# Transposes in two row halves, values in three pieces, a sixth query/key buffer and a new list

## The chip, the cores and the metric

The kernel runs on one core of a Trainium2 chip. The metric is the device time of one execution in microseconds (us), as the median of several runs; lower is better.

## The reference, cut to what matters

Causal attention on 4 batches of 12 heads (448 tokens, head size 64), and behind it a mixer: a product over tokens with a ReLU, added to x, then a product over channels with a ReLU, added again. All in 32-bit floats.

```python
def _attn_ref(q, k, v):
    scores = scale * np.matmul(q, k.transpose(0, 1, 3, 2))
    mask = np.triu(np.ones((seq, seq), dtype=bool), k=1)
    scores = np.where(mask, -1000000000.0, scores)
    scores = scores - np.max(scores, axis=-1, keepdims=True)
    attn = np.exp(scores)
    attn = attn / (np.sum(attn, axis=-1, keepdims=True) + 1e-09)
    return np.matmul(attn, v).astype(np.float32)

def _moe_ref(x, w_tok1, w_tok2, w_ch1, w_ch2):
    xt = x.transpose(0, 2, 1)
    h = np.maximum(xt @ w_tok1, 0.0) @ w_tok2
    u = x + h.transpose(0, 2, 1)
    h2 = np.maximum(u @ w_ch1, 0.0) @ w_ch2
    return (u + h2).astype(np.float32)
```

The 48 heads are taken as 24 pairs; x is 448 x 768 for a batch, w_tok1 448 x 256, w_ch1 768 x 1536.

## The kernel before, in words

**Attention.** For each of the 24 pairs: load q, k and v (SP's queue), transpose q and k in blocks (DVE), scores (TensorE, L958, both heads of the pair on row and column halves of the array), mask and maximum (DVE, L980), exponent with its sum (ACT, L992), scale by the reciprocal (POOL, DVE or ACT, L628 and L626), transpose the probabilities, multiply by v (TensorE, L1146 and, for the last 64 rows of keys, L1153, here called tips), and copy the result to u (`utile`, transposed: head size on the partitions). Rows of queries are handled in blocks of 64, grouped into four rounds (`ROUND`), two of which make a row group (`RG`). `probs` holds the probabilities of a round.

**Transposes.** The first ten pairs (`TURN = 10`) transpose their probabilities on TensorE (`by_tensor`, L1049): per round three or four squares of 128 x 128 into one PSUM bank, then one copy to `pt` (ACT or DVE). Two rounds hold their heads crossed and use an identity with its halves swapped, `across_ident`. The other 14 pairs use DMA transposes (`by_dma`, L1101), which this change leaves as they are. `xturn` (L1195) transposes u back for the product over tokens: per pair four squares into one bank, then a copy to `xh` and the remainder to `xl`.

**Mixer.** Products in fp32r with each operand split in a leading part and a remainder, three matmuls for one: over tokens L1243 and L1276, over channels L1326 and later L1654, L1725 and L1745. Products over channels of earlier batches stand between the attention of later ones.

**What sets the order.** `Plan` takes every piece of work as a job with a cost per engine, what it needs and what it holds. `emit` walks through a planned time and gives each engine the ready job with the lowest rank. The rank is taken from a table by name and pair (`PLACES`), the engine, where there is a choice, from another (`CHOICE`). PSUM banks are lent by kinds with a share each (`SHARE`: "s" scores, "t" transposes, "a" values, "m" mixer). Where TensorE has nothing ready in the first 75 us of planned time and was not busy enough just before, the plan puts in a filler, a matmul on the mask into a bank nobody reads (L854). Each engine then runs its list strictly in order, so a filler's time is spent whatever the others do. Where the way that TensorE's array is divided changes from one job to the next (`tiled`), the plan adds `SWITCH` ns.

**Buffers.** `kq` holds raw and transposed q and k, in five buffers; a load on SP's queue (L880) needs a free one.

## Time and profile before

| what | us |
|---|---|
| median of 3 runs | 548.14 (546.58 to 548.21) |
| the profiled execution, whole | 546.4 |
| its span, first to last instruction | 544.6 |
| TensorE busy | 535.3 |
| VectorE (DVE) busy | 426.5 |
| ScalarE (ACT) busy | 327.2 |
| GpSimd (POOL) busy | 147.8 |

Busy means that at least one instruction of the engine runs. TensorE's matmuls overlap: one's recorded duration is from its start to its last result, and the next starts long before that, so the pace is the distance of starts. Line numbers are those of the kernel before; in the changed kernel L958 is L957, L1049 is L1051, L1146 is L1167, L1153 is L1176, L1195 is L1213, L1326 is L1355 and L854 is L853.

### The profile page before, as it was taken

Reading aid. Unit: us, or ns where it says so; the run is one execution under the profiler, and the core shown is the slowest. Engines: PE = TensorE matmul, PEld = TensorE weight load, DVE = VectorE, ACT = ScalarE, POOL = GpSimd, SP = SyncE. Lnnn points to the kernel's source line nnn. Section 1 sums busy time; section 2 is a strip of 40 time slices with the busy share of each in tenths; the row PEclk is TensorE's granted clock in tenths of the full one; section 3 lists DMA queues with packets and bytes.
Section 4 is the critical chain, followed back from the end, with each engine's and each line's share of the span. In section 5 each row is a group of like instructions: output and inputs, shape, how many; then the busy total and the mean of one; then the engine's idle time right before and its main releaser. Section 6 shows DMA issues by size and latency. Waiting matters only on the chain.

```text
span 544.6 us, 11173 instructions
## 1 busy us (share of the span) xinstructions
PE 535.3 (98%) x3908; PEld 460.4 (85%) x3913; DVE 426.5 (78%) x1048; ACT 327.2 (60%) x786; POOL 147.8 (27%) x186
## 2 busy tenths in 40 slices
PE   8999999999999999999999999999999999999996
PEld 3678887888879888888877989999999999999995
DVE  5999888988796898687868798369987758476764
ACT  4999988889997796788758853154232314131300
POOL 2355844345233222203213010062201112221200
PEclk9999999999999999999999999999999999999999
DMA  6777777899899999999899745248632111212138
GB/s 111 148 172 148 180 173 163 215 201 176 188 190 194 199 213 178 200 179 177 193 191 196 190 130 161 77 109 162 130 89 73 45 60 57 65 52 88 29 62 142
DMA packets 231784, 77.69 MB, mean 143 GB/s; under 512 B 206000, under 2 KB 221232, under 8 KB 231728
## 3 DMA queue, kind: packets, MB, share of 16 engines
q1 hardware_dynamic: 220112, 75.37, 63.4%
q10 hardware_dynamic: 11616, 1.61, 1.7%
q8 instruction: 31, 0.51, 0.4%
q14 instruction: 25, 0.20, 0.2%
HBM read 49.15 MB, written 14.94 MB: 118 GB/s over the span
## 4 chain that ended last, share of the span: by engine, by line
PE 87%; DMA 6%; ACT 3%; SPq 2%; DVE 1%; issue 1%; ACTq 0%; POOL 0%; DVEq 0%; POOLq 0%
PE ps L1326 29%; PE ps L1745 14%; PE ps L1654 12%; PE ps L958 7%; PE ps L1146 6%; PE ps L1243 5%; PE ps L1276 5%; PE ps L1049 3%; PE ps L1725 3%; DMA out_dram<-kq 2%; PE ps L1195 2%; DMA pt<-prob 2%; SPq L880 2%; PE ps L1153 2%; PE ps L854 1%; ACT prob L992 1%
## 5 line engine op out<-in xcount | busy, mean ns | idle before, releaser
L1393 DVE TENSOR_TENSOR u<-ps,u 128x448 f32<-128x448 f32 x118 | 72.6, 618 | 38.9 <-PE ps L1745 25.5
L992 ACT ACTIVATE prob<-prob,stat 128x256 f32<-128x256 f32 (+6 forms) x168 | 83.6, 501 | 12.5 <-DVE stat L980 12.2
L637 POOL TENSOR_TENSOR wl<-wf,wh 128x768 fp32r<-128x768 f32 x22 | 41.4, 1883 | 99.1 <-ACT wh L626 71.4
L980 DVE CUSTOM_DVE_ANT_0 prob<-ps,mask 128x128 f32<-128x128 f32 (+6 forms) x168 | 63.2, 414 | 4.9 <-PE ps L958 4.5
L1326 PE MATMUL ps<-uh,wh 128*128 128x448 f32 x144 | 54.4, 378 | 0.0
L1326 PE MATMUL ps<-gh,wl 128*128 128x448 f32 x144 | 52.9, 367 | 1.2 <-POOL wl L637 1.2
L1326 PE MATMUL ps<-gh,wh 128*128 128x448 f32 x144 | 53.5, 372 | 0.0
L1326 PE MATMUL ps<-uh,wl 128*128 128x448 f32 x144 | 52.7, 366 | 0.1
L1326 PE MATMUL ps<-ul,wh 128*128 128x448 f32 x144 | 52.6, 365 | 0.0
L1326 PE MATMUL ps<-gl,wh 128*128 128x448 f32 x144 | 52.6, 365 | 0.0
L626 ACT ACTIVATE wh<-wf 128x768 fp32r<-128x768 f32 x26 | 21.6, 843 | 51.0 <-PE ps L1745 22.6
L628 POOL TENSOR_SCALAR prob<-prob,stat 128x384 f32<-128x384 f32 (+6 forms) x62 | 35.5, 580 | 60.5 <-DVE stat L1014 46.8
L958 PE MATMUL ps<-kq,kq 64*64 64x128 f32 (+5 forms) x768 | 46.6, 359 | 1.3 <-DVE stat L1011 0.8
L958 PEld LDWEIGHTS ps<-kq,kq 64*64 64x64 f32 x768 | 26.6, 133 | 20.8 <-issue 12.6
L632 ACT COPY pt<-pt 128x384 uint16<-128x384 uint16 (+3 forms) x45 | 36.1, 851 | 5.2 <-DMA pt<-prob 5.2
L1146 PE MATMUL ps<-pt,vraw 128*64 128x128 f32 (+1 forms) x384 | 37.2, 333 | 0.1
L1146 PEld LDWEIGHTS ps<-pt,vraw 128*64 128x64 f32 x384 | 23.7, 136 | 11.7 <-issue 2.4
L628 POOL TENSOR_SCALAR wh<-wf 128x768 fp32r<-128x768 f32 x16 | 14.0, 876 | 70.2 <-DVE wf L696 57.2
L686 ACT ACTIVATE wf<-wraw 128x768 f32<-128x768 f32 x24 | 21.9, 911 | 17.8 <-DMA wraw<-in_moe_w_ch_dram 17.4
L632 ACT COPY prob<-prob 128x1024 uint16<-128x1024 uint16 (+1 forms) x33 | 31.0, 950 | 2.0 <-DMA pt<-prob 1.1
L992 ACT ACTIVATION_READ_ACCUMULATOR prob<-prob,stat 128x1 f32 x168 | 32.0, 191 | 0.0
L1745 PE MATMUL ps<-u,wh 128*128 128x448 f32 x108 | 30.7, 365 | 0.0
(217 smaller groups left out, 1436.4 us busy)
## 6 DMA issues: line engine op xcount, KB each, us to landing
wraw<-in_moe_w_ch_dram SPq DMA_DIRECT2D x24, 768.0 KB, 5.5
wf<-scratch SPq DMA_DIRECT2D x30, 384.0 KB, 3.4
scratch<-wf SPq DMA_DIRECT2D x24, 384.0 KB, 4.4
vraw<-in_v_dram SPq DMA_DIRECT2D x48, 96.0 KB, 2.8
kq<-in_k_dram SPq DMA_DIRECT2D x60, 56.0 KB, 3.2
kq<-in_q_dram SPq DMA_DIRECT2D x56, 56.0 KB, 3.9
gh<-in_k_dram SPq DMA_DIRECT2D x36, 56.0 KB, 2.6
gl<-in_q_dram SPq DMA_DIRECT2D x36, 56.0 KB, 2.5
```

The lines of the kernel that those rows point to most:

```text
L628: eng[e].tensor_scalar(dst, src, scale, 0.0, op0=ALU.mult, op1=ALU.add)
L632: nc.scalar.copy(out, in_)
L637: eng[e].tensor_tensor(dst, a, b, op=ALU.subtract)
L958: nc.tensor.matmul(scores[n].tile[lanes, to:at], lhsT=qe.tile[LANES[j], c * QC:(c + 1) * QC], rhs=ke.tile[LANES[j], slice(*keys)], start=T ...
L980: nc.vector.tensor_tensor_reduce(out=part(c, r), in0=ps.tile[:, at:at + wide(c)], in1=mask[:, S - QC:S + P] if c == 2 else mask[:, S - wid ...
L992: nc.scalar.activation(part(c, r), part(c, r), AF.Exp, bias=stat.tile[:, 0, AT[c]:AT[c] + 1], scale=-1.0, accum_out=stat.tile[:, 1, AT[c]: ...
L1146: nc.tensor.matmul((low if c == 1 else ps).tile[LANES[j], c * QC:(c + nq) * QC], lhsT=s.tile[:, kb, j], rhs=view[:, o, 1 - j if c in MIXED ...
L1243: nc.tensor.matmul(ps.tile[:, :PART], lhsT=w[:, c, m * P:(m + 1) * P], rhs=x.tile[:, c, :], start=(n == 0), stop=(n == len(work) - 1),)
L1326: nc.tensor.matmul(ps.tile[:, :S], lhsT=x.tile[:, at_:at_ + P], rhs=y, start=(n == 0 and i == 0), stop=(n + 1 == w[2] and i == 2),)
L1393: eng[e].tensor_tensor(u, ps.tile[:, :S], u, op=ALU.add)
L1654: nc.tensor.matmul(ps.tile[:, :S], lhsT=l()[:, t * P:(t + 1) * P], rhs=r, start=(t == 0 and n == 0), stop=(t == half - 1 and n == 2),)
L1745: nc.tensor.matmul(ps.tile[:, :S], lhsT=l.tile[:, t * P:(t + 1) * P], rhs=r.tile, start=(n == 0), stop=(n == 3 * len(fs) - 1),)
```

## The change

**Transposes.** `by_tensor` now transposes a row group at a time, seven squares. Each square is two transposes of 64 rows and 128 columns, one on the upper and one on the lower row half of the array, into two PSUM banks; the crossed identity goes, since a half's place in `pt` now tells which head it is. Two copies follow, one for each bank, 448 columns each. `xturn` does the same for two pairs of u at once: eight squares, 16 half transposes, two banks, then two copies and two remainders. "t" may hold four banks.

**Values.** The job of a pair's values becomes three jobs: two of matmuls and one of tips. For the first ten pairs the new layout of `pt` cuts the columns differently (`PIECES`): eight matmuls per head and pair with two or one block of 64 queries each, where there were four with four or two.

**Buffers and plan.** `kq` gets a sixth buffer. `tiled` tells four ways of dividing the array apart instead of two, `SWITCH` is 95, and both tables are new. Of them the diff shows one row.

```diff
-    "by_tensor.flip": {0: (36, 40, 63, 72), 2: (77, 89, 92, 118), 4: (122, 141, 156, 166), 6: (170, 185, 207, 225),
...
+    "by_tensor.flip": {0: (39, 60), 2: (81, 88), 4: (128, 151), 6: (186, 195), 8: (259, 283), 10: (363, 374), 12:
+        (388, 421), 14: (470, 489), 16: (534, 549), 18: (544, 569)},
...
-    LEAD, SWITCH, RING, LANDS = 1400.0, 100.0, 128.0, (1400.0, 1000.0)
+    LEAD, SWITCH, RING, LANDS = 1400.0, 95.0, 128.0, (1400.0, 1000.0)
...
-    BUFS = {"wraw": 1, "wf": 2, "wh": 2, "wl": 2, "kq": 5, "vraw": 2, "vend": 2, "pt": 2}
+    BUFS = {"wraw": 1, "wf": 2, "wh": 2, "wl": 2, "kq": 6, "vraw": 2, "vend": 2, "pt": 2}
...
-    SHARE = {"s": 4, "t": 2, "a": 2, "m": 3, "w": 5}
+    SHARE = {"s": 4, "t": 4, "a": 2, "m": 3, "w": 5}
...
-    across_ident = const.tile([P, P], F32, name="across_ident")
-    for o in (0, P // 2):
-        nc.gpsimd.tensor_copy(across_ident[:, o:o + P // 2], ident[:, P // 2 - o:P - o])
...
+    FLAT = (7, 0)
+    PIECES = ((0, 0, 3, 3, 2, 4, 3), (0, 0, 4, 1, 2, 0, 11), (1, 0, 1, 1, 1, 6, 1), (1, 0, 2, 1, 1, 3, 1),
+              (0, 1, 3, 3, 2, 5, 3), (0, 1, 4, 1, 2, 1, 11), (0, 2, 5, 1, 1, 13, 1), (0, 2, 6, 1, 1, 9, 1))
+    TIPS = {15: 10, 9: 2}
...
-        prev = None
-        for r, cs in enumerate(ROUND):
+        for rg, at in zip(RG, FLAT):
...
-            ps = share("t")
...
-                        across_ident if r in CROSS else ident,
...
+            for r in rg:
+                for c in ROUND[r]:
...
+            both = share("t"), share("t")
+            squares = [(r, o) for r in rg for o in range(WIDTH[r])]
+            n = len(squares)
+            def flip(e, both=both, squares=squares):
+                for ps in both:
+                    bank(ps)
+                for k, (r, o) in enumerate(squares):
+                    for ps, rows in zip(both, LANES):
+                        nc.tensor.transpose(
+                            ps.tile[:, k * QC:(k + 1) * QC], probs[r].tile[rows, o * P:(o + 1) * P], ident[rows, rows]
+                        )
+            a = plan.job(
+                {"pe": 50.0 + 58.0 * n}, flip, norms, [*both, pt] + [probs[r] for r in rg], rank, tiled=3, turn=True
+            )
+            for h, ps in enumerate(both):
+                def evac(e, h=h, ps=ps, at=at, n=n):
+                    if pt.tile is None:
+                        make(pt, [P, 2, 2 * n, QC], F32)
+                    copy(e, pt.tile[:, h, at:at + n], ps.tile[:, :n * QC].rearrange("p (o q) -> p o q", q=QC))
+                done.append(plan.job({"act": act_ps(n * QC), "dve": dve1(n * QC)}, evac, [a], [ps, pt], rank))
...
+        banks = ps, low
+        flat_ = g < TURN
+        def chunks(n, j):
+            if flat_:
+                which, kb, c, step, nq, o, stride = PIECES[n]
+                out = banks[which].tile[LANES[j]].rearrange("p (c q) -> p c q", q=QC)[:, c:c + step * (nq - 1) + 1:step]
+                rhs = pt.tile[:, 1 - j if c in OVER else j, o:o + stride * (nq - 1) + 1:stride]
+                return kb, out, rhs
+            kb, o, c, nq = SUMS[n]
+            view = pt.tile.rearrange("p o (j q) -> p o j q", j=2)
+            return kb, banks[c == 1].tile[LANES[j], c * QC:(c + nq) * QC], view[:, o, 1 - j if c in MIXED else j]
+        def tip(o, c, j, half):
+            if flat_:
+                return pt.tile[LANES[half], 1 - j if c in OVER else j, TIPS[o]]
+            return pt.tile.rearrange("p o (j q) -> p o j q", j=2)[LANES[half], o, 1 - j if c in MIXED else j]
+        first_of = (0, 2) if flat_ else (0, 1)
...
-        for part in (range(2), range(2, 4)):
+        for part in ((range(4), range(4, 8)) if flat_ else (range(2), range(2, 4))):
...
+                        kb, to, rhs = chunks(n, j)
+                        nc.tensor.matmul(to, lhsT=s.tile[:, kb, j], rhs=rhs, start=(n in first_of), stop=False)
+            prev = plan.job(
+                {"pe": 650.0 if part[0] else 690.0}, pv, js + pdone + [prev], [ps, low, s, ends, pt, u], rank, tiled=1
+            )
+        def tips(e):
+            for half, kb, o, c in ENDS:
+                for j in range(2):
+                    nc.tensor.matmul(
+                        banks[half].tile[LANES[j], c * QC:(c + 1) * QC],
+                        lhsT=(ends if half else s).tile[LANES[half], kb, j], rhs=tip(o, c, j, half),
+                        start=False, stop=(o == 9),
+                    )
+        prev = plan.job({"pe": 265.0}, tips, [prev], [ps, low, s, ends, pt, u], rank, tiled=2)
...
+        if o < NTH - 1:
+            return
...
-                nc.tensor.transpose(ps.tile[:, c * P:(c + 1) * P], utile[b].tile[:, t, at:at + P], ident)
...
+        sh, sl = slot("xh"), slot("xl")
+        both = share("t"), share("t")
+        n = NCH * NTH * QC
...
+            for i in range(NTH):
+                for c in range(NCH):
+                    at = min(c * P, S - P)
+                    for ps, rows in zip(both, LANES):
+                        to = (i * NCH + c) * QC
+                        nc.tensor.transpose(
+                            ps.tile[:, to:to + QC], utile[b].tile[rows, t - o + i, at:at + P], ident[rows, rows]
+                        )
+        def src(h):
+            return both[h].tile[:, :n].rearrange("p (i c d) -> p i c d", i=NTH, c=NCH)
+        def view(x, h):
+            if x.tile is None:
+                make(x, [P, NCH, PART], F32R)
+            return x.tile.rearrange("p c (i h d) -> p i c h d", i=NTH, h=2)[:, :, :, h]
+        a = plan.job(
+            {"pe": 50.0 + 58.0 * NCH * NTH}, turn, [u_ready[b, t - i] for i in range(NTH)], [*both, utile[b]], rank,
+            tiled=3, turn=True,
+        )
+        done = []
+        for h, ps in enumerate(both):
+            def hi(e, h=h):
+                copy(e, view(sh, h), src(h))
+            def lo(e, h=h):
+                minus(e, view(sl, h), src(h), view(sh, h).bitcast(F32))
+            c = plan.job({"act": act_ps(n), "dve": dve1(n)}, hi, [a], [ps, sh], rank)
+            done += [c, plan.job({"dve": dve1(n)}, lo, [c], [ps, sh, sl], rank)]
...
```

Counted over the whole program, TensorE's matmuls on 236 squares become 472 halves, the fillers are 56 instead of 42, and the six other groups of matmuls keep their columns. Six weight remainders (`wl`, L637) go from POOL to DVE.

How the order moves. On TensorE, behind the last of the second product over tokens (`w2hi`, `w2lo` are its weights, `h1h`, `h1l` its input, `prob` the probabilities, `kq` the transposed q and k, `u` the attention's result), the kernel before has

```order
L1276 MATMUL ps_1022<-w2hi,h1h_902 128x448 x2
L1276 MATMUL ps_1022<-w2lo,h1h_902 128x448 x2
L1276 MATMUL ps_1022<-w2hi,h1l_916 128x448 x2
L1049 MATMUL ps_1037<-across_ident,prob_1_94 128x128 x4
L958 MATMUL ps_1045<-kq_991,kq_1020 64x448 x2
L958 MATMUL ps_1046<-kq_991,kq_1020 64x384 x2
L958 MATMUL ps_1046<-kq_991,kq_1020 64x64 x2
L1049 MATMUL ps_1061<-ident,prob_1_95 128x128 x3
L1195 MATMUL ps_1067<-ident,u_408 128x128 x4
```

and the changed kernel, with the flip's 14 rows cut to the first and last two,

```order
L1305 MATMUL ps_1133<-w2lo,h1h_1045 128x448 x2
L1305 MATMUL ps_1133<-w2hi,h1l_1070 128x448 x2
L1051 MATMUL ps_1156<-ident,prob_1_89 128x64
L1051 MATMUL ps_1157<-ident,prob_1_89 128x64
...
L1051 MATMUL ps_1156<-ident,prob_1_90 128x64
L1051 MATMUL ps_1157<-ident,prob_1_90 128x64
L957 MATMUL ps_1176<-kq_1142,kq_1153 64x448 x2
L957 MATMUL ps_1177<-kq_1142,kq_1153 64x384 x2
```

Before, each round's squares stand by themselves between the mixer's matmuls and the halves of a pair's scores, and the squares of u stand near. Now one row group stands as one block of 14 halves, on two banks in turn, with an array divided differently from that of its neighbours on both sides.

On TensorE, around the first squares of u, the kernel before has

```order
L958 MATMUL ps_428<-kq_299,kq_386 64x128 x2
L1195 MATMUL ps_452<-ident,u_408 128x128 x4
L1146 MATMUL ps_460<-pt_337,vraw_98 64x256 x2
L1146 MATMUL ps_461<-pt_337,vraw_98 64x128 x2
L1049 MATMUL ps_469<-across_ident,prob_0_89 128x128 x3
L1146 MATMUL ps_460<-pt_337,vraw_98 64x256 x2
```

and the changed kernel, where repeated rows, six of the seven fillers among them, are left out,

```order
L1051 MATMUL ps_547<-ident,prob_0_88 128x64
L1051 MATMUL ps_548<-ident,prob_0_88 128x64
L853 LDWEIGHTS mask
L853 MATMUL ps_84<-mask 128x512
...
L1213 MATMUL ps_595<-ident,u_446 128x64
L1213 MATMUL ps_596<-ident,u_446 128x64
...
L957 MATMUL ps_615<-kq_570,kq_591 64x448 x2
L957 MATMUL ps_616<-kq_570,kq_591 64x384 x2
```

Before, the squares of u follow scores directly, and the values of the next pair, cut in two by a flip, follow them. Now a flip and seven fillers (LDWEIGHTS and MATMUL on `mask`) stand ahead of the squares of u, which come for two pairs in one block of 16 halves, and scores follow.

## Rows read from the trace of the kernel before

**Rows 1.** The page: span, TensorE's busy time, share of the chain by engine.

```profile
span 544.6 us, 11173 instructions
...
PE 535.3 (98%) x3908; PEld 460.4 (85%) x3913; DVE 426.5 (78%) x1048; ACT 327.2 (60%) x786; POOL 147.8 (27%) x186
...
PE 87%; DMA 6%; ACT 3%; SPq 2%; DVE 1%; issue 1%; ACTq 0%; POOL 0%; DVEq 0%; POOLq 0%
```

**Rows 2.** Windows: stretch, length, busy us by engine, clock, DMA share, GB/s.

```profile
0.00:40.00 40.00, 37.02 (x381) 23.43 (x387) 32.55 (x127) 32.05 (x104) 14.38 (x39) 1.00 0.73 144
40.00:80.00 40.00, 40.00 (x450) 32.48 (x451) 35.98 (x118) 37.30 (x119) 25.64 (x40) 1.00 0.77 166
...
240.00:280.00 40.00, 38.77 (x330) 32.19 (x326) 30.89 (x80) 26.49 (x63) 9.47 (x14) 1.00 0.90 182
...
520.00:545.00 25.00, 20.20 (x102) 18.12 (x100) 13.70 (x25) 0.77 (x2) 0.00 (x0) 0.99 0.65 111
```

**Rows 3.** Groups of TensorE by form: busy us, mean ns, idle before.

```profile
L854 PE MATMUL ps<-mask 128*128 128x512 bf16 x37 | 11.3, 437 | 1.7 <-POOL mask L647 1.5
```

**Rows 4.** Timeline of TensorE, 90 to 96.4 us: start us, length us, line, form, count.

```profile
90.14 0.60 PE L1195 MATMUL ps<-ident,u 128*128 128x128 f32 x4
90.49 0.45 PE L1326 MATMUL ps<-uh,wh 128*128 128x448 f32 x1
90.78 0.37 PE L1326 MATMUL ps<-ul,wh 128*128 128x448 f32 x1
90.99 0.36 PE L1326 MATMUL ps<-uh,wl 128*128 128x448 f32 x1
...
93.34 0.60 PE L1049 MATMUL ps<-across_ident,prob 128*128 128x128 f32 x4
93.87 1.52 PE L1146 MATMUL ps<-pt,vraw 128*64 128x256 f32 x16
95.33 0.27 PE L1153 MATMUL ps<-pt,vraw 64*64 64x64 f32 x2
95.34 0.27 PE L1153 MATMUL ps<-pt,vend 64*64 64x64 f32 x2
95.43 0.22 PE L1153 MATMUL ps<-pt,vraw 64*64 64x64 f32 x2
...
95.55 0.23 PE L1153 MATMUL ps<-pt,vraw 64*64 64x64 f32 x2
...
95.72 0.47 PE L1326 MATMUL ps<-uh,wh 128*128 128x448 f32 x1
96.03 0.36 PE L1326 MATMUL ps<-ul,wh 128*128 128x448 f32 x1
```

**Rows 5.** Timeline of TensorE, 17 to 19 us and 29.5 to 31 us.

```profile
17.34 0.98 PE L1049 MATMUL ps<-ident,prob 128*128 128x128 f32 x7
18.26 1.05 PE L958 MATMUL ps<-kq,kq 64*64 64x320 f32 x20
...
29.62 0.38 PE L854 MATMUL ps<-mask 128*128 128x512 bf16 x1
...
30.27 0.81 PE L854 MATMUL ps<-mask 128*128 128x512 bf16 x3
```

**Rows 6.** Instructions of lines L1049, L1153, L1326: duration ns minimum/median/maximum.

```profile
L1049 PE MATMUL ps<-ident,prob x70: 272/273/331, 12.0 to 99.8; 128*128 128x128 f32 x70
...
L1153 PE MATMUL ps<-pt,vraw x192: 217/218/268, 21.8 to 323.1; 64*64 64x64 f32 x192
...
L1326 PE MATMUL ps<-uh,wh x144: 362/365/472, 63.5 to 358.7; 128*128 128x448 f32 x144
```

**Rows 7.** Waits of TensorE: for what, us in total, times, longest.

```profile
PE ps L854 <- POOL mask L647: 1.5, 1, 1.5
PE ps L1326 <- POOL wl L637: 1.2, 1, 1.2
PE ps L958 <- DVE stat L1011: 0.8, 1, 0.8
PE ps L958 <- DVE u L1284: 0.5, 1, 0.5
```

383 lines of the change are left out of this document (163 added, 220 removed), and 224 rows, old and new, of tables (CHOICE, PLACES).

## The prediction

> **What bounds the kernel now.** I read the page's first part and its chain first: TensorE is busy 98% of the span and carries 87% of the chain that ended last [rows 1]. The windows say the same by stage: it is full from 40 to 80 us, and the only open stretches are the first 40 us (2.98 us short, 1.49 of them before the first instruction), the stretch from 240 to 280 us (1.2 us short) and the last 25 us, where the output drains [rows 2]. The list of waits names three of importance, together 2.5 us [rows 7]. So the time is a sum of steps on TensorE, and the other engines count only where they make it wait. A share of this busy time is not the kernel's work: matmuls on the mask (L854), which the planner puts in while nothing else is ready [rows 3].
>
> How long a step is must be read from one start to the next, since the durations overlap: a transpose lasts 0.27 us, but four of them that end 0.60 us after the first start stand (0.60 - 0.273) / 3 = 0.109 us apart [rows 4, 6]. In the same way an fp32r matmul of 448 columns takes 0.20 us [rows 4], a filler (0.81 - 0.38) / 2 = 0.215 us, its length of 0.38 us being that of the single one in the row before [rows 5], and the 64-row tips two rounds in 0.12 us, each round four matmuls side by side on four quarters of the array, on two row halves and two banks at once; I take 0.058 us a round [rows 4].
>
> **Halved transposes.** Before there are 140 squares of probabilities and 96 of u, 236 x 0.109 = 25.7 us. Now each square is two transposes of 64 rows, with 64 identity columns instead of 128, on the two row halves. No row shows a transpose on a part of the array. Upper bound: the halves don't overlap, 0.109 us a square, nothing gained. Lower bound: 64 of 128 columns at the pace of now, 0.054 us. I take 0.058 us, the pace of the tips, which also move 64 columns, also load weights before each, and also write two banks from two row halves. 236 x 0.058 = 13.7 us, so **-12.0 us**.
>
> The weights could set a slower pace, since each half still loads 128 columns. What a load takes shows where it isn't hidden, on the first matmul after another tiling: its duration is longer than the median by the load. That is 331 - 273 = 58 ns for a transpose (128 columns), 268 - 218 = 50 ns for a tip (64 columns), 472 - 365 = 107 ns for an fp32r matmul (128 columns) [rows 6]. The transpose loads its 128 columns in 58 ns, so the pace I took stands. The Trainium skill (TensorE: Matmul & The Clock Gate, section "LDWEIGHTS (loading the stationary operand)") says that a load takes its columns divided by 1.2, in ns, however few rows it has; that fits the tip and the fp32r load, but would be 107 ns for a transpose, and this trace shows 58. By that rule the halves could not go below 107 ns a square and this term would be nearly nothing; that is a rival below.
>
> **Changes of tiling.** A full transpose uses the array as the fp32r matmuls do, and costs nothing extra among them: from the last of four transposes (start 90.14 + 3 x 0.109 = 90.47) to the second matmul after them it is 0.31 us, just 0.109 + 0.20 [rows 4]. A halved one has a tiling of its own. What a change costs: from the last transpose (93.67) to the first values matmul 0.20 us instead of 0.109, so 0.09, and a load of 0.05 to 0.06 that isn't hidden [rows 4, 6]: 0.15 us into a tiled piece or into a transpose after one. Check: seven transposes between two score pieces take 0.92 us, which is 7 x 0.109 + 0.16 [rows 5]. Into fp32r matmuls it is 0.09 and a load of 0.107: from the last round of tips at 95.55 to the second matmul at 96.03 it is 0.48 us instead of 0.06 + 0.20 [rows 4, 6], so 0.20 us; into a filler I take 0.10, the drain alone.
> I counted the changes in the order of the instructions. Before: 117, of which 98 go into a tiled piece or a transpose, 18 into fp32r matmuls, 1 into a filler: 98 x 0.15 + 18 x 0.20 + 0.1 = 18.4 us. Now: 155, of which 102, 41 and 12: 15.3 + 8.2 + 1.2 = 24.7 us. **+6.3 us.** Where a flip of seven squares stands between fp32r matmuls it gains nothing: 7 x 0.058 + 0.15 + 0.20 = 0.76 us against 7 x 0.109 = 0.76. The gain comes from those beside scores, values and each other.
>
> **Values in three pieces.** One pair's values take 1.46 us now [rows 4], of which 0.16 are load and drain; 1.30 us are eight steps, four of 256 columns (0.216) and four of 128 (0.109). For the first ten pairs they become eight of 128 and eight of 64: 8 x 0.109 + 8 x 0.058 = 1.34 us. **+0.4 us** for ten pairs; the cuts after part and tips are in the count of changes.
>
> **Fillers.** 42 before, 56 now, by count in the order (the trace recorded 37 of the 42 [rows 3]). TensorE runs its queue in order, so 14 x 0.215 = **+3.0 us** are spent whether anything is late or not. They all stand in the first part, where the squares of probabilities are: a good part of what the flips give back there goes to fillers.
>
> **What costs nothing.** The copies out of PSUM keep their elements: four a pair for the probabilities, of 448 columns instead of 512 and 384, and the same columns for u; ACT and DVE do them beside TensorE. The two POOL copies for the crossed identity go; the first filler waits for the mask (1.5 us [rows 7]), which is made before them. The sixth query/key buffer lets one load be issued earlier on SP's queue; who could gain is the wait for POOL's weight split, 1.2 us [rows 7], at most.
>
> **Waits under the new list.** Every job has a new place, so where TensorE waits is open. Bounds: at best the 2.5 us of [rows 7] and some smaller ones go, -4 us; at worst as much again comes, +4 us. I take 0, since both lists are made by the same planner from nearly the same costs.
>
> Sum: -12.0 + 6.3 + 0.4 + 3.0 = **-2.3 us**. The profiled execution has a span of 544.6 us [rows 1] in 546.4 us; the median of the runs is 548.1, so the same step gives 548.1 - 2.3 = **545.8 us**.
>
> **Rivals.** (1) *The new list closes the waits.* TensorE loses 2.5 us to named waits and some small ones; with these gone, 545.8 - 4 = 541.8 us. For it: the sixth buffer, and the six weight splits that go from POOL to DVE. Against it: two of the three waits are one-off meetings with DVE.
> (2) *The gain upstream turns into waits.* TensorE gets to each softmax earlier, and DVE and ACT, 36 and 37 us busy of 40 between 40 and 80 us [rows 2], do not get faster; a flip now also needs the scaled rows of two rounds instead of one, and two banks, and scores queued behind it wait with it. Of the 12.0 us, 140 x 0.051 = 7.1 are won in that part, and the fillers take 3.0 of them. If the other 4.1 us are waited away too, the result is 545.8 + 4.1 = 549.9, just slower; if half of them, 547.9, no change. Against it: before, this part has full windows with one wait of 0.5 us.
> (3) *The weight load sets the pace of the halves: slower.* If a half transpose loads its 128 columns as an fp32r matmul does, in 107 ns, and that is not hidden by 64 columns, a square costs 0.107 us, the first term shrinks to 236 x 0.002 = 0.5 us, and the sum is +9.2: 557.3 us. It decides from 0.068 us a square on, where 236 x 0.010 eats the 2.3 us. Against it: the 58 ns of the full transpose [rows 6].
> (4) *The halves do not run side by side*, so the change doesn't do what it says: again 0.109 us a square, 557.8 us, the same place in the sum. Against it: the tips' four quarters.
>
> **How the numbers follow.** Forecast 0.60, with 543 to 549 of its own for the waits; rival 1 0.12, rival 2 0.19, rivals 3 and 4 together 0.09. The range must hold 8 in 10: 541.0 takes in rival 1, 551.0 the worst bound of the waits; what is left out is rivals 3 and 4 and the ends. About 0.3% (1.6 us) is what a measurement of this kernel can tell from no change: faster is below 546.5, slower above 549.8. From the forecast about two thirds lie below 546.5 (0.40), with rival 1 faster has 0.52; same has 0.18 of the forecast and 0.12 of rival 2, 0.30; slower has 0.09 of rivals 3 and 4, 0.02 of the forecast and 0.07 of rival 2, 0.18.
>
> **What would show it.** Transposes of the new lines some 0.058 us apart by pairs, and 14 of them in 0.41 us: right; 0.75 us: rival 3 or 4. First matmuls after a flip 0.2 us late: the term for tilings is right. Waits on TensorE in the new list of waits: if they add up to 5 us or more, rival 2; to under 1 us, rival 1. I would be wrong altogether if a halved transpose costs more than the full one, or if the span's last stage, untouched here, changes.

## The result, and the profile after the change

| | before | after |
|---|---|---|
| median of 20 runs each, us | 546.49 (543.57 to 549.21) | 549.51 (546.72 to 553.29) |
| ratio after / before | | 1.006, 95% interval 1.0039 to 1.008 |
| span of the profiled execution, us | 544.6 | 550.1 |
| start of TensorE's first to start of its last matmul, us | 1.5 to 540.0 | 1.5 to 545.8 |

The change makes the kernel 3.0 us slower, where 2.3 us faster was forecast. 549.5 us lies inside the range, but only because the three runs of before that the forecast started from were 1.7 us above the median of twenty and the range was wide; the sign is wrong.

The page of after (span, busy time by engine, chain by engine) answers to [rows 1]. TensorE's busy share is 98% as before, but it carries 72% of the chain, where it was 87%.

```profile
span 550.1 us, 11963 instructions
...
PE 536.8 (98%) x4323; PEld 459.1 (83%) x4323; DVE 432.6 (79%) x1049; ACT 320.0 (58%) x769; POOL 147.6 (27%) x200
...
PE 72%; DMA 6%; ACT 5%; SPq 3%; DVE 2%; issue 1%; DVEq 0%; ACTq 0%
```

The windows of after (stretch, length, busy us by engine, clock, DMA share, GB/s) answer to [rows 2]. The first 40 us are 1.4 us emptier than before. TensorE was full from 40 to 80 us and is now 2.1 us short there; from 160 to 240 us, where it was full too (two rows of before, then five of after), it is 2.0 us short. Only the stretch from 240 to 280 us got clearly better, by 1.2 us.

```profile
160.00:200.00 40.00, 40.00 (x341) 34.32 (x334) 31.52 (x93) 32.29 (x77) 11.92 (x13) 1.00 1.03 205
200.00:240.00 40.00, 40.00 (x317) 35.00 (x319) 31.26 (x84) 32.13 (x74) 8.69 (x12) 1.00 0.93 198
```

```profile
0.00:40.00 40.00, 35.65 (x496) 21.85 (x497) 31.30 (x123) 31.04 (x103) 15.72 (x39) 1.00 0.70 137
40.00:80.00 40.00, 37.91 (x547) 29.43 (x547) 34.30 (x113) 33.30 (x104) 22.21 (x39) 1.00 0.75 163
...
160.00:200.00 40.00, 38.90 (x358) 31.63 (x357) 33.16 (x89) 31.31 (x73) 8.73 (x14) 1.00 0.93 185
200.00:240.00 40.00, 39.06 (x302) 33.35 (x301) 33.88 (x97) 32.44 (x80) 10.34 (x14) 1.00 0.97 185
240.00:280.00 40.00, 40.00 (x340) 33.81 (x340) 35.68 (x94) 27.72 (x62) 6.97 (x11) 1.00 0.98 206
```

**TensorE's own steps came as forecast.** In this timeline of TensorE in after (start us, length us, line, form, count) a flip of 14 halves and a turn of 16 halves of u follow each other.

```profile
69.28 0.37 PE L1355 MATMUL ps<-uh,wl 128*128 128x448 f32 x1
69.58 0.65 PE L1051 MATMUL ps<-ident,prob 64*128 64x64 f32 x14
70.06 0.67 PE L1213 MATMUL ps<-ident,u 64*128 64x64 f32 x16
70.66 0.99 PE L957 MATMUL ps<-kq,kq 64*64 64x448 f32 x12
```

A flip behind tips that waits for nothing needs 0.58 us for its 14 halves, from the last start of the tips to its own last start (behind most scores it is 0.63). Less 0.15 for the change of tiling, 0.58 gives 0.43 / 7 = 0.0615 us a square; 0.058 was forecast. The second fp32r matmul behind a halved flip starts 0.46 us after the flip's last start. The flip's own last step (0.06) and one matmul (0.20) would give 0.26, so the change costs 0.20, as forecast. The values of one of the first ten pairs, up to the next step, take 1.488 us for 1.451, ten times 0.037. So the sum of own steps is 236 x (0.0615 - 0.109) = -11.2, +6.3, +0.4, +3.0: -1.5 us. But TensorE's stretch from first to last matmul grew by 5.8 us in this execution, so its waits, taken as what is left, grew by 7.3 us. A second profiled execution of the same kernel (further below) ended 2.1 us earlier: 5.2 us of waits.

The groups of TensorE by form (busy us, mean ns, idle before) answer to [rows 3]: 56 fillers, and the 472 halves.

```profile
L853 PE MATMUL ps<-mask 128*128 128x512 bf16 x56 | 15.8, 414 | 1.5 <-POOL mask L642 1.5
L1051 PE MATMUL ps<-ident,prob 64*128 64x64 f32 x280 | 13.5, 230 | 1.5 <-POOL stat L1010 0.8 <-ACT pt L624 0.5
L1213 PE MATMUL ps<-ident,u 64*128 64x64 f32 x192 | 8.8, 229 | 0.1
```

The list of TensorE's waits in after (for what, us in total, times, longest) answers to [rows 7]. It names only the longer gaps, 8.8 us in all where before has 4.3, and shows many small meetings instead of a few large ones. Its longest lines:

```profile
PE ps L957 <- DVE kq L924: 2.2, 2, 1.5
PE ps L853 <- POOL mask L642: 1.5, 1, 1.5
PE ps L1051 <- POOL stat L1010: 0.8, 1, 0.8
PE ps L1167 <- ACT pt L630: 0.8, 3, 0.3
PE ps L1167 <- DVE pt L632: 0.7, 1, 0.7
PE ps L1355 <- DVE stat L979: 0.6, 1, 0.6
```

**The largest new wait leads to SP's queue.** The scores of pair 7 (L957) wait for the transposed k of that pair (DVE, L924), and DVE waited 2.36 us for its load to land. DVE's and TensorE's rows in after:

```profile
59.93 0.65 DVE L924 STREAM_TRANSPOSE kq<-gh 128x448 f32<-128x448 f32 x1 [2.36 <-DMA gh<-in_k_dram]
...
61.16 0.59 PE L957 MATMUL ps<-kq,kq 64*64 64x448 f32 x2 [1.50 <-DVE kq L924]
```

These are the rows of SP's own queue (start, time in the queue, line, what is loaded, DMAs), first of before. There the eighth load of k, pair 7's, is issued at 44.95 us.

```profile
40.69 1.89 SPq L880 DMA_DIRECT2D gh<-in_k_dram  x4
42.62 0.48 SPq L683 DMA_DIRECT2D wraw<-in_moe_w_ch_dram  x1
43.21 1.01 SPq L889 DMA_DIRECT2D vraw<-in_v_dram  x2
44.27 0.62 SPq L893 DMA_DIRECT2D vraw<-in_v_dram  x1
44.95 2.72 SPq L880 DMA_DIRECT2D gh<-in_k_dram  x4
```

In after it is issued at 53.81 us, behind two loads of q and one of v:

```profile
43.81 2.74 SPq L879 DMA_DIRECT2D gh<-in_k_dram  x4
46.72 5.33 SPq L879 DMA_DIRECT2D gl<-in_q_dram  x8
52.16 0.94 SPq L888 DMA_DIRECT2D vraw<-in_v_dram  x2
53.15 0.61 SPq L892 DMA_DIRECT2D vraw<-in_v_dram  x1
53.81 5.68 SPq L879 DMA_DIRECT2D gh<-in_k_dram  x8
```

Neither queue has a gap to speak of. From 1.7 to 75 us one DMA is issued behind the other, some 0.48 us each and more where the queue is held up; the longest pause is 0.45 us before and 0.51 after. None of this stands in [rows 1 to 7], which have the share of the DMA engines (0.73 and 0.77, [rows 2]), and the prediction has no term for the queue. Its lateness can be followed to the first DMA transpose, pair 10's. It is issued at 99.35 us before and at 102.98 us after:

```profile
99.35 1.35 SPq L1101 DMA_TRANSPOSE pt<-prob  x1
```

```profile
102.98 2.33 SPq L1102 DMA_TRANSPOSE pt<-prob  x1
```

From there to the last matmul it is 540.0 - 99.4 = 440.6 us before and 545.8 - 103.0 = 442.8 us after. So of 5.8 us, 3.6 are lost ahead of that point. This pair of numbers serves as a yardstick below.

**The plan and the chip.** While the kernel is built, the planner computes a time for every job. Its last job ends at 535.7 us before and at 532.6 us after: the new list is 3.1 us better in the plan. The end of each pair's tips on the chip, less the planned time, in us:

| pair | 0 | 2 | 5 | 7 | 9 | 13 | 17 | 23 |
|---|---|---|---|---|---|---|---|---|
| before | -0.5 | 0.0 | -0.1 | 0.2 | 1.5 | 2.6 | 2.9 | 5.8 |
| after | -0.1 | 1.2 | 3.6 | 5.3 | 6.7 | 9.4 | 11.7 | 14.0 |

The list of before meets its plan within 0.5 us for 80 us; the new one falls behind from the third pair on.

The planner has times for the loads too. Before, each load of q and k on SP's queue up to 69 us is issued within 0.1 us of its planned time or ahead of it, by up to 1.8 us. After, they fall behind from the fifth load of k on (24.05 us, 22.77 planned), and by 67.9 us they are 6.0 us late. Of the 8.9 us by which pair 7's k is issued later than before, 4.5 are the new list's choice (planned at 46.73 and at 51.26 us); the rest is this falling behind. In the first 75 us SP's queue itself waits 7.3 us for others before and 4.5 after. So before, its loads had a little room; after, they have less.

### The profile page after: what moved, and what is told of

Read it like the earlier page. It is cut to its first block, busy times and chain, and to the rows that moved or that the text cites. A ratio compares the mean times of both kernels' runs of the same rounds, so it can differ in the third digit from the quotient of the medians.

```text
span 550.1 us, 11963 instructions
## 1 busy us (share of the span) xinstructions
PE 536.8 (98%) x4323; PEld 459.1 (83%) x4323; DVE 432.6 (79%) x1049; ACT 320.0 (58%) x769; POOL 147.6 (27%) x200
## 4 chain that ended last, share of the span: by engine, by line
PE 72%; DMA 6%; ACT 5%; SPq 3%; DVE 2%; issue 1%; DVEq 0%; ACTq 0%
PE ps L1355 25%; PE ps L1774 16%; PE ps L1683 12%; PE ps L1167 4%; PE ps L1272 3%; PE ps L957 3%; PE ps L1305 3%; DMA wraw<-in_moe_w_ch_dram 3%; PE ps L1754 3%; SPq L879 2%; DMA pt<-prob 2%; ACT pt L630 1%; ACT prob L991 1%; PE ps L1176 1%; PE ps L1213 1%
## 5 line engine op out<-in xcount | busy, mean ns | idle before, releaser
L991 ACT ACTIVATE prob<-prob,stat 128x384 f32<-128x384 f32 (+6 forms) x168 | 83.8, 502 | 19.4 <-DVE stat L979 19.1
L979 DVE CUSTOM_DVE_ANT_0 prob<-ps,mask 128x384 f32<-128x384 f32 (+6 forms) x168 | 63.2, 414 | 4.3 <-PE ps L957 3.8
L626 POOL TENSOR_SCALAR prob<-prob,stat 128x384 f32<-128x384 f32 (+6 forms) x76 | 40.5, 543 | 78.3 <-DVE stat L1013 76.0
L635 POOL TENSOR_TENSOR wl<-wf,wh 128x768 fp32r<-128x768 f32 x16 | 30.6, 1914 | 68.8 <-ACT wh L624 50.8
L957 PE MATMUL ps<-kq,kq 64*64 64x128 f32 (+5 forms) x768 | 45.8, 358 | 2.9 <-DVE kq L924 2.2
L630 ACT COPY pt<-pt 128x512 uint16<-128x512 uint16 (+3 forms) x52 | 42.6, 882 | 6.5 <-DMA pt<-prob 6.5
L957 PEld LDWEIGHTS ps<-kq,kq 64*64 64x64 f32 x768 | 26.5, 133 | 21.6 <-issue 10.9
L1167 PE MATMUL ps<-pt,vraw 128*64 128x128 f32 (+2 forms) x544 | 38.5, 284 | 1.5 <-ACT pt L630 0.8
L1167 PEld LDWEIGHTS ps<-pt,vraw 128*64 128x64 f32 x544 | 29.8, 137 | 11.1 <-ACT pt L630 2.1
L635 POOL TENSOR_TENSOR ul<-u,uh 128x448 fp32r<-128x448 f32 x18 | 24.5, 1377 | 26.6 <-DVE uh L626 20.5
L1355 PEld LDWEIGHTS ps<-uh,wh 128*128 128x128 f32 x144 | 27.0, 188 | 3.8 <-issue 1.1
```

The lines of the kernel that those rows point to most:

```text
L626: eng[e].tensor_scalar(dst, src, scale, 0.0, op0=ALU.mult, op1=ALU.add)
L630: nc.scalar.copy(out, in_)
L635: eng[e].tensor_tensor(dst, a, b, op=ALU.subtract)
L957: nc.tensor.matmul(scores[n].tile[lanes, to:at], lhsT=qe.tile[LANES[j], c * QC:(c + 1) * QC], rhs=ke.tile[LANES[j], slice(*keys)], start=T ...
L979: nc.vector.tensor_tensor_reduce(out=part(c, r), in0=ps.tile[:, at:at + wide(c)], in1=mask[:, S - QC:S + P] if c == 2 else mask[:, S - wid ...
L991: nc.scalar.activation(part(c, r), part(c, r), AF.Exp, bias=stat.tile[:, 0, AT[c]:AT[c] + 1], scale=-1.0, accum_out=stat.tile[:, 1, AT[c]: ...
```

## The experiments

Three theories were set against each other at first. **A**: the new list was fitted to a plan that runs ahead of the chip. **B**: the structure makes the waits, since a flip now needs two rounds and two banks. **C**: other engines set the pace where the transposes stand. The first results made **S** of C: it is SP's queue of loads that sets the pace. All ratios are to the kernel before, run beside it on the same chip.

### Measured prices in the planner

```diff
-                    end += self.SWITCH * (pick.tiled != tiled)
+                    end += (0.0 if pick.tiled == tiled else 200.0 if pick.tiled == 0 else 130.0)
...
-                        free[e] = now + self.filler.costs[e] * (2.0 if now < 4000.0 else 1.0)
+                        free[e] = now + self.filler.costs[e] * (2.0 if now < 4000.0 else 1.0) + 100.0 * (tiled != 0)
+                        tiled = 0
```

> The changed kernel with one edit in the planner: a change of tiling is priced as the traces show it, 200 ns into fp32r matmuls, 130 ns into a tiled step, 100 ns ahead of a filler, where it was 95 ns for all and nothing ahead of a filler. The ranks stay, so TensorE's own steps stay too (154 changes for 155, 51 fillers for 56, together 1.1 us less). Theory A (the list is fitted to a plan that runs ahead of the chip, so TensorE meets inputs that are not there yet): with the right prices the plan falls behind as the chip does, work is picked by what is there, and the 13 us of waits fall to 8 or less: ratio to the kernel before 0.994 to 1.000, 543 to 546.5 us. Theory B (the new structure, flips that need two rounds and two banks, makes the waits) and theory C (DVE, ACT and the loads set the pace): the waits stay over 11 us, ratio 1.003 to 1.007.

Measured: 551.75 us, ratio 1.009 (1.0057 to 1.0122). The plan now ends at 542.1 us instead of 532.6, so some 9.5 of the 14 us by which the chip falls behind are prices of TensorE's own steps that were too low (an estimate, since the prices also move a few places in the order). But the chip is no faster: pair 10's first DMA transpose comes at 104.2 us. Theory A in the form that right prices alone mend the order falls. That a list fitted again to right prices would be better was not tried, and the planned times of the loads were not touched.

### Whole squares in the same order

```diff
-                    for ps, rows in zip(both, LANES):
-                        nc.tensor.transpose(
-                            ps.tile[:, k * QC:(k + 1) * QC], probs[r].tile[rows, o * P:(o + 1) * P], ident[rows, rows]
-                        )
+                    at = k % 4 * P
+                    nc.tensor.transpose(
+                        both[k // 4].tile[:, at:at + P], probs[r].tile[:, o * P:(o + 1) * P], ident
+                    )
...
-                    for ps, rows in zip(both, LANES):
-                        to = (i * NCH + c) * QC
-                        nc.tensor.transpose(
-                            ps.tile[:, to:to + QC], utile[b].tile[rows, t - o + i, at:at + P], ident[rows, rows]
-                        )
+                    nc.tensor.transpose(
+                        both[i].tile[:, c * P:(c + 1) * P], utile[b].tile[:, t - o + i, at:at + P], ident
+                    )
```

> The changed kernel with whole 128x128 transposes again, in the same jobs, the same two banks and the same order on every engine: squares 0 to 3 go to one bank and 4 to 6 to the other. TensorE's own steps get 236 x (0.109 - 0.0615) = 11.2 us longer and lose 38 changes of tiling (6.0 us by 0.15, 0.20 and 0.10): +5.2 us. Theory C (other engines set the pace where the transposes stand, so the halves' gain is waited away): less than half of it shows, ratio to the kernel before 1.005 to 1.010. Theories A and B (the transposes are on the path, the waits have other causes): all of it shows, ratio 1.013 to 1.018, 553.5 to 556 us.

Measured: 547.39 us, ratio 1.0028 (1.001 to 1.0045). TensorE has 5.2 us more of its own to do (4.6 us when the squares are compared place by place in the traces, three places where halves wait included), and the kernel is 0.3% faster than with halves, below what any theory allowed. In the list of waits nearly all small meetings are gone:

```profile
PE ps L853 <- POOL mask L642: 1.5, 1, 1.5
PE ps L1051 <- POOL stat L1010: 0.8, 1, 0.8
PE ps L957 <- DVE kq L924: 0.7, 1, 0.7
PE ps L1171 <- ACT gh L1389: 0.6, 1, 0.6
PE ps L957 <- DVE stat L1013: 0.3, 1, 0.3
```

So the halves' gain was not on the path; and something about them costs. This run also speaks against theory B. It keeps the new list, the sixth buffer and flips of two rounds and two banks. Its own steps are -1.5 + 5.2 = 3.7 us above those of before and its time 1.4 us, so by the same sum it waits 2.3 us less than before.

### Fewer fillers, after and before

```diff
-                        self.filler.fn(e)
+                        if now < 8000.0:
+                            self.filler.fn(e)
```

> The changed kernel with the same order but 42 of its 56 fillers left out (those after 8 us of planned time). Own steps lose 42 x 0.215 + 2 = 11 us. If fillers are on the path, as the prediction had it (3.0 us for 14 more): ratio to the kernel before 0.986 to 0.990. If they stand in time that would be waited away anyhow (theory C): the waits grow by what the fillers give back, ratio 1.003 to 1.008. A lower granted clock in the first 60 us would add time; it is told by the windows.

> The kernel before with the same order but 28 of its 42 fillers left out (those after 8 us of planned time), 6 us of TensorE's own time. The premise of the prediction (the time is the sum of TensorE's steps): ratio 0.987 to 0.992. Theory S: TensorE waits for what the fillers covered, ratio 0.997 to 1.003.

Measured: after without 42 fillers 549.89 us, ratio 1.0072 (1.0047 to 1.0097); before without 28 fillers 547.03 us, ratio 1.0009 (0.9988 to 1.0031). Neither is faster. The windows of the first 40 us, first of after, then of before, each without the fillers, show what took their place: TensorE stands open for 9.1 and 7.7 us, and its granted clock falls to a mean of 0.87 and 0.96 (1.00 is the upper level, 2.4 GHz).

```profile
0.00:40.00 40.00, 30.94 (x462) 21.31 (x463) 30.62 (x123) 31.16 (x103) 15.32 (x38) 0.87 0.71 141
```

```profile
0.00:40.00 40.00, 32.33 (x343) 20.18 (x344) 30.75 (x121) 30.20 (x98) 14.49 (x39) 0.96 0.71 143
```

The lower clock takes something back: (1 - 0.87) x 40 = 5.2 us and 1.6 us of work at full speed, an estimate from these rows. Of the 11 and 6 us of own time that were left out, that still leaves some 6 and 4 us that went away without the end coming nearer. So TensorE isn't the bound where these fillers stand: up to 72 us after, and up to 34 us before, since all 42 fillers of before start between 1.5 and 34.3 us.

The full windows of before [rows 2] begin behind them. From 40 to 80 us before has no filler, and it is nearly as full without the fillers ahead:

```profile
40.00:80.00 40.00, 39.67 (x439) 32.34 (x438) 36.02 (x117) 37.81 (x120) 25.47 (x41) 1.00 0.76 164
```

No run took work from TensorE in that stretch of before, so that it isn't the bound there is not shown. There is a little room behind it: with fewer fillers the tips of pair 7 come 2.2 us later than before (84.3 for 82.1 us) and those of pair 8 only 1.0 us (96.5 for 95.6).

### The list of before under the new steps

```diff
-    "by_tensor.flip": {0: (39, 60), 2: (81, 88), 4: (128, 151), 6: (186, 195), 8: (259, 283), 10: (363, 374), 12:
...
+    "by_tensor.flip": {0: (40, 72), 2: (89, 118), 4: (141, 166), 6: (185, 225), 8: (295, 324), 10: (357, 385),
...
```

> The changed kernel's steps (halves, values in three pieces, sixth buffer) under the ranks and choices of the kernel before: a flip of two rounds takes the later round's rank, the tips stand right behind the second half of the values, the squares of two pairs of u stand at the second pair's place. Own steps: 156 changes, 57 fillers, like the changed kernel. Theory A (the newly fitted list is the cause): waits as in the kernel before, about 6 us, so 549.5 - 7 = 542.5, up to 546.5 for what does not fit, ratio 0.993 to 1.000. Theory B (flips that wait for two rounds make the waits whatever the list): waits of 12 us or more, ratio 1.005 or above, and they stand ahead of flips and of the scores behind them.

> The changed kernel's steps under the ranks of the kernel before, as in the run with halves (1.0075), but with whole squares, in that run's order. Own steps 11.2 us more and 43 changes (6.8 us) less, +4.4 us. If halves cost time wherever other engines and loads set the pace: ratio 1.003 to 1.007. If the whole squares' gain belongs to the new list alone: 1.010 to 1.016.

Measured: with halves 550.36 us, ratio 1.0075 (1.0045 to 1.0104); with whole squares 549.96 us, ratio 1.0062 (1.0037 to 1.0087). The first lies where B expected it (1.005 or above), and its longest new wait, 1.9 us, is that of a flip. But the two decide little between A and B: a list that was not fitted to its steps loses by that alone (the plan ends at 539.8 us), and these ranks were not. They do repeat one thing: 4.4 us more of own steps show as nothing here too.

### More and less on SP's queue

Twenty small loads more (the last rows of v a second and a third time, into DRAM that nobody reads), 0.60 us each in the queue:

```diff
...
+                for x in spent if g < 10 else ():
+                    nc.sync.dma_start(out=x[:], in_=src[b, 2 * t:2 * t + 2, full * P:].rearrange("h p d -> p h d"))
```

> The changed kernel with two more small loads on SP's queue behind each of the first ten loads of v (the last rows of v again, into DRAM that nobody reads): 20 issues of about 0.6 us, 12 us of SP's queue in the first 80 us, in the same order on every engine otherwise. Theory S (SP's queue of loads, which issues without a gap from 1.7 to 75 us, sets the pace of the first part, not TensorE): 8 to 12 us show, ratio to the kernel before 1.020 to 1.030. If TensorE's steps set the pace and the loads have room: under 3 us show, ratio 1.004 to 1.011.

> The kernel before with the same 20 small loads on SP's queue, its order kept otherwise. Theory S in the strong form (SP's queue sets the pace of the first part before the change too, so that nothing won on TensorE there can show): 6 to 12 us show, ratio 1.011 to 1.022. If the kernel before is bound by TensorE there, as the prediction had it: ratio 0.998 to 1.004.

Measured: after 559.24 us, ratio 1.0233 (1.0206 to 1.026), 9.5 us more than the changed kernel by the ratios; before 557.52 us, ratio 1.0202 (1.0175 to 1.023), 11 us more than the kernel before. Of 12 us in the queue nearly all show. In before with the extra loads TensorE is no longer full from 40 to 80 us, and pair 10's first DMA transpose moves from 99.35 to 109.81 us:

```profile
40.00:80.00 40.00, 36.61 (x395) 29.40 (x396) 31.34 (x106) 32.91 (x105) 21.72 (x33) 0.96 0.69 147
...
L898 SPq DMA_DIRECT2D spent<-in_v_dram x20: 594/601/1367, 15.2 to 96.1; - x20
...
109.81 1.35 SPq L1104 DMA_TRANSPOSE pt<-prob  x1
```

Both lie where theory S expected them. The Trainium skill (DMA: Bandwidth & Descriptors, section "Issuing engines are not separate DMA queues") says that issuing on more engines saves only the time that the sequencer takes to initiate a DMA, usually small beside the DMA itself. For a single DMA the traces agree: 0.48 to 0.60 us in SP's queue, where an early load of k lands 2.6 us and a load of weights (`wraw`) 5.6 us after its issue (medians). But 114 of them stand one behind the other and fill 67 of the first 75 us of the queue after, and the twenty loads make this sum longer.

The loads of v for pairs 1 to 9 on GpSimd's queue:

```diff
+                queue = nc.gpsimd if 0 < g < 10 else nc.sync
...
-                    nc.sync.dma_start(
+                    queue.dma_start(
...
```

> The changed kernel with the loads of v for pairs 1 to 9 issued on GpSimd's queue instead of SP's (27 DMAs, some 16 us of SP's queue), the order kept otherwise. Theory S: the loads of q and k come earlier, TensorE's waits in the first 100 us (about 7 us) fall to 3 or less: 543 to 546 us, ratio 0.994 to 1.001. If the loads don't matter: 1.004 to 1.008. If the issuing holds up GpSimd's scaling of probabilities: 1.009 or more, with waits on GpSimd's prob ahead of flips.

> The kernel before with the loads of v for pairs 1 to 9 issued on GpSimd's queue. Its order has fixed fillers and few waits, so Theory S gives little by itself: ratio 0.994 to 1.000. If GpSimd is held up by the issuing: 1.003 or more.

Measured: 551.54 us, ratio 1.0087 (1.0064 to 1.0111), and 551.67 us, ratio 1.0096 (1.0064 to 1.0128). SP's queue did get ahead (pair 7's k at 47.1 instead of 53.8 us, and the wait for L924 fell from 2.2 to 0.6 us), but each load of v holds GpSimd for 2.2 us, and GpSimd scales the probabilities late. In after with this edit the first line of TensorE's waits is now

```profile
PE ps L1052 <- POOL prob L626: 2.9, 2, 2.2
```

The loads of q for pairs 1 and 2 on ScalarE's queue, which has nothing else to do before 8 us:

```diff
+                queue = nc.scalar if src is q and g in (1, 2) else eng[e]
...
-                    eng[e].dma_start(
+                    queue.dma_start(
```

> The changed kernel with the loads of q for pairs 1 and 2 (eight DMAs, 4 us of SP's queue between 5 and 9 us) issued on ScalarE's queue, where nothing else stands before 8 us; every engine's order is kept otherwise. Theory S (the pace of SP's queue sets the first part): all later loads come up to 4 us sooner, so 2 to 4 us are won: ratio to the kernel before 0.998 to 1.002. If what limits the loads is how soon transfers land and not where they are issued, or TensorE sets the pace: 1.004 to 1.008.

> The kernel before with the same eight loads of q issued on ScalarE's queue. Theory S in the strong form (SP's queue also bounds the first part of the kernel before): 2 to 4 us won, ratio 0.992 to 0.997, faster than both kernels. If TensorE bounds it there: 0.998 to 1.002.

Measured: after 547.46 us, ratio 1.002 (0.9992 to 1.0048); before 546.62 us, ratio 1.0011 (0.9991 to 1.0031). The changed kernel gains some 2 us (the unchanged one, beside it on the same chip, is at 1.0058; the intervals overlap), and pair 10's first DMA transpose comes at 98.5 us. The kernel before gains nothing, so the strong form of S holds in one direction only. Why shows in the waits of SP's own queue in its first 90 us:

```profile
SPq L683 <- DVE wf L696: 4.4, 4, 1.5
SPq L881 <- PE ps L959: 4.3, 2, 2.7
```

A queue that is 4 us early waits 4.4 us for the weights' buffers, which DVE frees (L696), and 4.3 us for TensorE's scores, where before the longest waits at these two lines are 1.8 and 1.7 us; by 40.7 us it is where it was. As far as these runs show, loads, buffers, softmax and TensorE move in step there. Loads that are 12 us later delay the end by 9.5 and 11 us; loads that are 4 us earlier before, or fillers that are gone, are waited away.

### The changed kernel once more

> The changed kernel once more, unchanged, for the run to run part of its waits: the same ratio, 1.004 to 1.008. If SP's queue sets the pace, the lateness of its loads (the fifth load of k at 24.0 us, pair 10's first DMA transpose at 103.0 us in the first profile) moves with the span from run to run; a span 3 us shorter would have that transpose about 2 us sooner.

Measured (no edit): 550.09 us, ratio 1.0058 (1.0026 to 1.0089); span 548.2 us, first DMA transpose at 101.47 us. Span and transpose moved together, by 1.9 and 1.5 us. The difference to before is the kernel's, and some 2 us of the profiled waits are the execution's.

### Which halves

With whole squares for the probabilities alone (the first half of the diff of the whole squares above), for u alone (its second half), and for both with the loads of q on ScalarE's queue:

> The changed kernel with whole 128x128 transposes for the probabilities alone (140 squares), halves kept for u, same order on every engine. Own steps: 140 x (0.109 - 0.0615) = 6.7 us more, some 2 to 4 us of changes less. Theory F (the halves of the probabilities are what costs, in the part where TensorE isn't the bound): ratio to the kernel before 1.001 to 1.004, as with all squares whole. Theory U (those of u are): ratio 1.005 to 1.009. If own steps are the time after all: 1.011 to 1.015.

> The changed kernel with whole transposes for u alone (96 squares), halves kept for the probabilities, same order. Own steps: 96 x (0.109 - 0.0615) = 4.6 us more, some 3 us of changes less. Theory U (with halves both banks are full only at the end, the first copy to xh starts 1.67 us after the first transpose instead of 1.12, and the products over tokens and what is queued behind the copies come later): ratio 1.001 to 1.004. Theory F: ratio 1.005 to 1.009.

> The changed kernel with all squares whole and the loads of q for pairs 1 and 2 on ScalarE's queue, same order. If the two gains seen singly add (1.006 to 1.003, and 1.006 to 1.002): ratio 0.997 to 1.001. If they take away the same wait: 1.001 to 1.004.

Measured: probabilities whole 549.44 us, ratio 1.0054 (1.0036 to 1.0073); u whole 546.48 us, ratio 1.0003 (0.998 to 1.0026); both whole with q on ScalarE 549.03 us, ratio 1.0044 (1.0023 to 1.0064). The halves of the probabilities are worth nothing that these runs can tell: 140 x 0.0475 = 6.7 us less 2.6 us of changes can be added, 4.1 us, and the time stays. The halves of u cost: without them, though TensorE has 96 x 0.0475 = 4.6 less 2.9 = 1.7 us more to do, the kernel is back at the time of before. The gains of whole squares and of q on ScalarE do not add.

Why u? One explanation was that with halves both banks are full only at the end, so the first copy to `xh` starts late (1.67 us after the first transpose, mean of 12; 1.12 with all squares whole, but 1.29 and 1.53 in two profiles of u whole). It can be tried by itself: u whole, but the eight squares written to the two banks in turn.

```diff
-            for i in range(NTH):
-                for c in range(NCH):
+            for c in range(NCH):
+                for i in range(NTH):
```

> The changed kernel with whole transposes for u, as in the run before, but the eight squares written to the two banks in turn (first pair, second pair, first pair ...) instead of the first pair's four and then the second pair's four. Same own steps, same order of jobs; only the first bank is full after seven squares instead of four, 0.33 us later. Theory L (halves of u cost because both banks come full at the end and the copies and what is queued behind them start late): ratio to the kernel before 1.003 to 1.007. If the gain of whole squares has another cause (no change of tiling around them): as the repeated run, 0.998 to 1.002.

> The changed kernel with whole transposes for u once more, unchanged, beside the run with the banks in turn. The first time gave 1.0003. If that was the kernel and not the runs' luck with the loads: ratio 0.998 to 1.003, with pair 10's first DMA transpose issued before 100.5 us; if it was luck: 1.004 to 1.007 and 101.5 us or later.

Measured: in turn 547.37 us, ratio 1.0016 (0.9989 to 1.0042); u whole again 547.97 us, ratio 1.0025 (0.9996 to 1.0053). The copies do start late again (1.74 us), and the time doesn't follow: this explanation isn't borne out. The repeat came out higher than the first time; the mean of the two is 1.0014, against 1.0059 of the changed kernel's two series, a difference of 0.0045 with an uncertainty of about 0.0025 from the four intervals. So whole squares of u win 1 to 4 us, and the mechanism stays open. The lists of waits show one meeting that goes with it. In the six profiles with the new list's order, halves of u and no extra loads, the values wait 0.4 to 2.8 us for DVE's copy of `pt` (L1167 <- DVE pt L632 in after); in the five with whole squares of u it is 0 to 0.4 us. What makes it no run shows.

The yardstick over the runs (in us; "rest" is from pair 10's first DMA transpose to the last matmul):

| kernel | ratio | first DMA transpose | rest |
|---|---|---|---|
| before | 1 | 99.4 | 440.6 |
| before, fewer fillers | 1.0009 | 100.1 | 439.5 |
| before, q on ScalarE | 1.0011 | 100.1 | 439.2 |
| before, v on GpSimd | 1.0096 | 106.9 | 438.6 |
| before, 20 loads more | 1.0202 | 109.8 | 439.9 |
| after, two executions | 1.006, 1.0058 | 103.0, 101.5 | 442.8, 442.2 |
| after, fewer fillers | 1.0072 | 100.7 | 442.1 |
| after, q on ScalarE | 1.002 | 98.5 | 442.1 |
| after, v on GpSimd | 1.0087 | 102.8 | 442.8 |
| after, probabilities whole | 1.0054 | 101.8 | 443.5 |
| after, u whole, two executions | 1.0003, 1.0025 | 98.7, 99.8 | 441.2, 441.3 |
| after, u whole, banks in turn | 1.0016 | 101.6 | 440.9 |
| after, all whole | 1.0028 | 101.3 | 440.4 |
| after, all whole, q on ScalarE | 1.0044 | 102.5 | 441.2 |

Two parts can be told apart: when the loads of the first part are through, which scatters by 1 to 2 us from one execution to the next, and the rest, 442.1 to 443.5 us with halves of u and 440.4 to 441.3 with whole ones. Each row is one execution, and in the order of before the rest runs from 438.6 to 440.6 us, so a single difference of 2 us is no proof by itself. The changed kernel with 20 loads more is an exception (113.1 and 440.2 us, with halves), and in the order of before's ranks the rest is the same either way (441.4 and 441.3).

## Why the prediction was wrong

**The step that failed** is the last term of the sum, waits under the new list: 0 taken, with -4 to +4 as bounds. It was +7.3 us in the profiled execution, +5.2 in the second, and 3.0 + 1.5 = 4.5 us by the medians. All three lie above the upper bound. It was bounded by what before loses to waits, although the trace of before shows nothing that limits waits that aren't there yet.

**Behind it stands a premise**, the first paragraph's: "So the time is a sum of steps on TensorE". For the first 100 us of the changed kernel it is refuted: 42 fillers can go, or 4.1 us of whole probabilities come, and the time stays. Of the kernel before it is refuted up to 34 us, where 28 fillers can go and nothing is won; behind that it is not shown either way, but 12 us on SP's queue cost 11, so its loads have little room. TensorE's busy share was read as a bound, while the 42 fillers [rows 3] said that it had nothing to do at times. (The stretch from 80 to 120 us, 0.5 us short, was left out of the open ones; no term hangs on it.) The term -12.0 had 7.1 us of its gain in the first part, where the runs show nothing of it.

**Point by point:**
- Halved transposes: the mechanism and the price were right, 0.0615 us a square for 0.058, -11.2 for -12.0 us. Rivals 3 and 4 fell. The rule of the Trainium skill cited there (TensorE: Matmul & The Clock Gate, "LDWEIGHTS (loading the stationary operand)"), by which a square of halves could not take less than 0.107 us, does not hold here.
- Changes of tiling: 0.15 and 0.20 us a change, as measured. Values: +0.4 us, right. Both on TensorE's own account.
- Fillers: 14 more, 3.0 us of TensorE's time, but no time of the kernel that a run could tell; "spent whether anything is late or not" holds for the engine only.
- "What costs nothing": the place of the loads was not costed. The prediction followed the sixth buffer one load forward and did not follow SP's queue, where pair 7's k went 8.9 us back, half of it by the list itself.
- Rival 2 was the nearest. Its sign and place (the first part, waits of 5 us or more) were right, its cause only in part: it named DVE's and ACT's busy time and the flip's two rounds; what the runs show is loads that fall behind their plan, in step with the other engines. That flips wait because they need two rounds was not shown by any run; with whole squares they still need them, and the sum leaves fewer waits than before.
- The last stage is unchanged, as forecast: from the last tips to the last matmul 221.1 us for 216.9, with 1087 of the mixer's matmuls in it for 1069, and 18 x 0.20 us are 3.6 of these 4.2 us.

**Not settled:** why halves of u cost time; whether TensorE bounds the kernel before from 40 to 100 us; and whether a list fitted to the measured prices would turn the new structure into a gain. No version ran faster than the kernel before; u whole with halved probabilities equals it.

## What to carry to other kernels

A busy engine is a bound only where taking work from it moves the end: count its fillers first, look where they stand, and try to remove a few before costing a speed-up of it. Read every queue of DMA issues row by row, with what it waits for: a queue without gaps can be a bound that no share of DMA time shows, and an early load's place in it is a term of the sum. A planner's list fits its own prices; lay its planned times, those of the loads too, beside the trace's, and where a new list runs ahead of the chip from the start, expect the difference to come back as waits.

## What the runs showed of the hardware

A transpose of 64 rows on either row half, two side by side into two PSUM banks, takes 0.0615 us for a 128x128 square where a whole one takes 0.109. A DMA issue that nothing holds up stays in its engine's queue some 0.5 to 0.8 us, and the larger transfer is not the longer one: 0.48 for 768 KB of weights and 0.60 for 32 KB of v on SP, 0.6 to 0.8 for v on GpSimd. And without 42 fillers, with TensorE open for 9.1 of the first 40 us, its granted clock there fell to a mean of 0.87, between the levels of 1.2 and 2.4 GHz; the time stayed within the noise (ratio 1.0072 for 1.006).
